# Nystromformer attention and a multiplicative feed-forward on one core: an earlier table load, constants split between two engines, later w_out loads on SyncE, and the first eighth of w3 x w_out in two kinds of products

## The chip, the core and the metric

The kernel runs on one core of a Trainium2 chip. The core has five engines with instruction streams of their own, which wait for each other through semaphores: TensorE (PE, matrix products), VectorE (DVE), ScalarE (ACT), GpSimd (POOL) and SyncE (SP, which issues loads and stores). The metric is the device time of one execution in microseconds; shorter is better.

## What is computed

Eight batches of eight heads with 576 rows of 64 go through a Nystrom attention with 32 landmarks; the result, as 4608 rows of 512, goes through a feed-forward in which two projections are multiplied.

```python
q_lm = q.reshape(B, H, m, S // m, D).mean(axis=3)      # m = 32 landmarks, S // m = 18 rows each
k_lm = k.reshape(B, H, m, S // m, D).mean(axis=3)
A, Bm, C = sm(q, k_lm), sm(q_lm, k_lm), sm(q_lm, k)    # softmax of scaled scores
Z = Bm.transpose(0, 1, 3, 2) / (norm1(Bm) * norm_inf(Bm) + 1e-06)
for _ in range(6):
    Z = 2 * Z - Z @ Bm @ Z
x = (A @ Z @ C @ v), heads side by side: 4608 x 512
a, b = x @ w1, x @ w2                                  # 512 -> 1024 each
out = ((a * b) @ w3) @ w_out                           # 1024 -> 1024 -> 512
```

The kernel forms w3 @ w_out (1024 x 512) once, so that each row then needs one product less.

## The kernel before, in words

**Tasks and an order written out.** The program is a list of some 1330 small tasks. Each has a name, an engine, a function that issues its instructions, and rings of buffers or banks that it takes and gives back. ORDER (L39 to L116) names every task once, with the buffer that it takes behind a colon; `run` (L149) issues the tasks in just that order. So ORDER fixes, for each engine, the sequence of its instructions: an engine that waits for one instruction does nothing that stands behind it. The costs and due times given with the tasks play no part any more once ORDER is written.

**The names.** The 64 heads are 16 quads n of four heads. Of a quad, `lq` n t (L599, GpSimd's queue) loads K (t = 0) and Q (t = 1); `T` (L429) transposes them on VectorE; the landmark means come from TensorE for quads 0 and 1 (`mp`, L450, with the identity `ident16`) and from GpSimd for the others (`ma`, `mb`); `mk` (L458) scales them on ScalarE, `lt` (L471) transposes them; `S` and `A` (L478, L527) are the scores, `sm`, `sw`, `sb`, `se`, `ct` and `ar`, `am`, `as`, `ae`, `au`, `an`, `aT` their softmax on VectorE, GpSimd and ScalarE. `sw` (L500) is a small matmul with the constant `swapneg`. Batches b of two quads then have `C`, `W`, `U`; groups i of batches have the iteration for Z (`N`, `x`, `y`, `Z`). `d`, `e`, `f` are the dense products of the feed-forward, `g`, `h`, `st` its end and the stores.

**w3 x w_out.** Both weights are split into a half-precision copy and a half-precision remainder, so that the product of the copies and two products of a copy with a remainder give the wanted exactness. w_out is loaded in four quarters `wf0` to `wf3` of four pieces each: the pieces marked s are issued by SyncE, those marked a by ScalarE (L380). Of each eighth c, `woh` (L312, ScalarE) is the copy and `wol` (L317, VectorE) the remainder. w3 comes in eight slabs `w3n` j of 512 KB; `tr` (L323) transposes half a slab into a PSUM bank, `wh` (L330, ScalarE) and `wl` (L337, VectorE) make copy and remainder. `mm` j c (L347) does the three products of slab j with eighth c, 192 matmuls of 512 columns in all, and `wo` j (L357) takes the sum out. The gates `gw` 0 to 3 (L363, GpSimd) copy one element of each w_out quarter; the loads of Q and K from quad 2 on and of w1 and w2 (`lw`) stand behind gw3, so that they start only when w_out is there.

**The start.** `zz` (L260) clears a tile, on which 30 warm-up matmuls (`wu0` to `wu4`, L263, six each) run. `ca`, `cb` and `cc` make the constants: `cb` on GpSimd the identity, `cc` (L272) on VectorE everything else in 24 instructions. On ScalarE the order is: the loads of w3n0a, wf0a, wf1a and the first piece of wf2a, then wh00, wh01, woh1, woh0, the second piece of wf2a, mk0, wf3a, woh2, woh3 and so on. ScalarE's table load stands ahead of its first activation, wh00. On VectorE: cc, tr00, T00, tr01, wl01, wl00, T01, wol0, wol1, lt0, T10, sm0, wol2, ar0. On TensorE: wu4, mp0, mm00, mm01, S0, A0, sw0, mm02, mp1, mm03.

The functions that the change touches, and what calls them, with the line numbers that the profile uses:

Of the kernel before, what the change touches and what calls it, by code (L numbers as in the profile page):

```python
# [39 lines left out]
w3n0a.0 w3n0.0:0 zz w3n0a w3n0 lq00:0 ca wu0:0 wf0a.0 wf0s.0 lq01 wf0a wf0s lq10:1 wf1a.0 wf1s.0 wf1a wf1s lq11  # L40
wf2a.0 wf2s.0 cb wf2s wu1:1 cc wf3s.0 wu2:2 wf3s tr00:3.0 wu3:4 T00:0 wh00 tr01:5 w3n1.0:1 wu4:6 wh01 wl01 woh1
gw0 w3n1.1 wl00 mp0:7 woh0 T01 wf2a wol0 mk0:0 w3n1.2 wol1 mm00:0 wf3a.0 mm01 lt0 wf3a T10:1 S0:1.2 woh2 gw1
w3n1 A0:4.6 sm0:0 woh3 wol2 sw0 ar0:0 mm02 w3n2.0:2 sb0 wol3 mp1:5 am0:1 woh4 gw2 w3n2.1 mm03 woh5 wol4 w3n2.2
mk1:1 T11 mm04 gw3 w3n2 wol5 as0 woh7 w3n3.0:0 lt1 woh6 mm05 wol7 w3n3.1 lq20:2 se00:0 A1:3.7 w3n3.2 wol6 ae0
lq21 w3n3 tr10:4.1 mm06 lq30:3 au0 wh10 lq31 S1:6.5 se01 mm07 lq40:0 wl10 lw10 tr11:1 mm10:2 lq41 ar1:1 wh11
w3n4.0:1 mm11 an0:0 w3n4.1 tr20:4.0 mm12 w3n4.2 am1:2 lw11 mm13 wh20 w3n4 bo0:0 wl11 lw00 T20:0 mm14 as1 wl20
mm15 sm1:3 mm20:3 ae1 ma2:0 tr21:7 mm16 ct0:0 sw1 w3n5.0:2 mm21 w3n5.1 sb1 T21 se10:1 mm17 w3n5.2 lq50:1 aT0:0
se11 mm22 w3n5 mb2 tr30:1.1 wh21 mm23 au1 wh30 wl21 bo1 N0:4.4 tr31:6 mm24 wl30 w3n6.0:0 lq51 mk2:0 mm25 w3n6.1
bt0 T30:1 lq60:2 mm26 w3n6.2 an1:1 no0:0 wh31 mm27 mm30:5 ct1:1 ma3:0 mm31 lt2 w3n6 wl31 A2:7.1 tr40:4.0 mm32
# [10 lines left out]
ct3:0 lv4 mb7 mm76 wq0 lv5.0:1 sb6 au5 se60:1 U000:3.7.0.1 lv5.1 U010:1.4 se61 lv5.2 am6:0 U011:2.5 uo0001 lv5  # L60
mm77 bo5 T71 uo0100 N1:6.3 uo0110 ct5:1 lq100:2 mk7:1 C1:7.1 bt1 an5:1 T80:0 no1:0 uo0111 ma8:0 uo0000 wo7 aT5:5
U001:2.5 lv6.0:2 lt7 co1:1.5 lv6.1 uo0011 S7:3.6 lv6.2 uo0101 sm7:1 as6 A7:0.5 lv6 uo0010 d010:1.7 lv7.0:3 T81
lv7.1 mb8 d000:4.2 ar7:1 e010:0 lv7.2 sw7 lv7 e000:1 T90:1 C2:1.0 ae6 am7:2 sb7 au6 lq101 mk8:0 f000:0 as7
x1_0:5 lv8.0:0 co2:0.3 d020:4.2 lv8.1 se70:0 lv8.2 lt8 lq110:3 d002:0.1 se71 y1_0:1 lv8 T91 ma9:0 e020:2
d030:3.5 lv9.0:1 e002:1 f010 lv9.1 x1_1:6 f002:1 e030:0 lv9.2 d011:4.0 f020 ae7 ct6:0 d012:7.1 bo6:0 an6:0
e011:1 y1_1:2 A8:3.2 e012:2 f030 d022:4.6 mb9 ar8:0 d032:7.5 f012 d001:2.3 e032:0 am8:6 e022:2 x1_2:1 f011
S8:7.4 y1_2:0 g00:0 f032 lq111 mk9:1 f022 lq120:0 x1_3:1 T100:0 lq121 d021:5.6 e001:1 sm8:8 ma10:0 g01 e021:0
f001 lt9 sw8 y1_3:1 d031:2.5 sb8 f021 se80:1 x1_4:3 T101 e031:2 S9:1.6 lq130:1 h0:0 au7 g30:7 mb10 st0.0 g31
y1_4:2 lv9 bo7 ct7:2 A9:2.0 h3:1 f031 Z1:3 se81 sm9:5 st3.0 g10:7 T110:1 an7:1 mk10:0 sw9 zo1:1 g11 as8 sb9
aT7:0 se90:0 lt10 W1:5 ar9:1 h1:2 W2:4 ma11:0 g20:3 wp1:1 ae8 wq1 T111 se91 U100:1.7.2.3 am9:4 wp2:0 g21 uo1000  # L70
aT6:1 uo1001 as9 wq2 U101:0.2 h2:3 ct9:1 U200:5.6.0.1 uo1010 au8 U210:1.7 mb11 uo2000 S10:4.3 uo2101 C3:0.5
sm10:9 ae9 bo8 ct8:3 uo2100 au9 uo2001 uo1011 an8:1 sw10 lv10.0:2 A10:7.1 mk11:1 co3:1.3 lv10.1 U211:6.2 lv10.2
sb10 an9:0 ar10:0 U111:0.5 uo2111 lv10 se100:0 lv11.0:3 am10:0 d200:2.1 ma12:0 bo9 lv11.1 uo1110 T120:0 d211:7.4
lv11.2 e200:1 lv11 se101 lt11 N2:0.2 T121 st1.0 uo2110 C4:2.3 bt2 uo1111 f200:2 as10 e211:0 no2:0 lq131 ae10
f211 mb12 U201:6.5 lv12.0:0 co4:0.1 U110:1.7 lv12.1 uo2010 A11:0.4 au10 lv12.2 uo2011 d201:2.3 lv12 uo1101
lv13.0:1 ar11:1 uo1100 d202:6.5 st2.0 d120:7.1 lq140:2 am11:7 e202:2 lv13.1 e201:1 lq141 st2 S11:0.4 f202:3
# [86 lines left out]
def kernel(  # L163
# [860 lines left out]
```

## Time and profile before

| | us |
|---|---|
| median of 3 runs | 271.43 (270.89 to 271.73) |
| profiled execution | 273.18 |
| its span, first to last instruction | 271.1 |
| TensorE busy | 256.1 |
| VectorE busy | 193.8 |
| ScalarE busy | 162.0 |
| GpSimd busy | 131.8 |

The loads move 37.33 MB in all; the mean granted TensorE clock is 0.986. In the rows of the profile PE is TensorE, PEld its weight loads, DVE VectorE, ACT ScalarE, POOL GpSimd, SP SyncE; a q behind a name is the engine's sequencer, which issues loads. Nearly all matmuls have line L243, that of a helper, so they are told apart by their tiles. The w_out quarters are loaded into tiles that later hold other things, and so are called u (wf0, wf1) and ab (wf2, wf3).

### The profile page before, as it was taken

What the parts mean: (1) busy time and instruction counts of PE and PEld (TensorE: products, weight loads), DVE (VectorE), ACT (ScalarE), POOL (GpSimd) and SP (SyncE); (2) the same over time, 40 slices, a digit from 0 to 9 for tenths busy, and PEclk for the clock granted to TensorE, in tenths of its full rate; (3) what the DMA queues carried; (4) which work ended last, traced back from release to release, by engine and by line L of the source; (5) the groups of instructions that cost most, each with busy time, mean ns of one, the idle gap of its engine ahead of it and who ended that gap; (6) DMA issues with size and microseconds to landing.
All of it is one profiled execution on the core that took longest, in us unless ns stands there. A gap on an engine that the chain in (4) does not pass through costs nothing.

```text
span 271.1 us, 9581 instructions
## 1 busy us (share of the span) xinstructions
PE 256.1 (94%) x3954; PEld 168.5 (62%) x3954; DVE 193.8 (71%) x470; ACT 162.0 (60%) x414; POOL 131.8 (49%) x147
## 2 busy tenths in 40 slices
PE   8569989999999999999999999999999999999992
PEld 3325434454558875679867556976857597666752
DVE  4659999999999999999899868744664076313330
ACT  0546364565576757989864898735024984593542
POOL 4007899999999999999788431000020000000000
PEclk9986999999999999999999999999999999999999
DMA  7998999999988967099643133023624050142455
GB/s 155 282 211 187 194 234 236 235 245 232 222 217 202 203 136 166 10 203 203 154 77 89 41 80 85 19 62 97 170 77 95 4 119 0 41 101 47 109 136 138
DMA packets 22668, 37.33 MB, mean 138 GB/s; under 512 B 3552, under 2 KB 7904, under 8 KB 22624
## 3 DMA queue, kind: packets, MB, share of 16 engines
q1 hardware_dynamic: 15920, 23.80, 34.9%
q0 software_dynamic: 5696, 11.54, 24.4%
q10 hardware_dynamic: 1008, 1.38, 1.8%
q8 instruction: 31, 0.51, 0.8%
q14 instruction: 13, 0.11, 0.1%
HBM read 38.80 MB, written 9.44 MB: 178 GB/s over the span
## 4 chain that ended last, share of the span: by engine, by line
PE 57%; DMA 15%; DVE 10%; POOL 10%; ACT 2%; issue 2%; SPq 1%; ACTq 0%; DVEq 0%; POOLq 0%
PE bank L243 57%; DMA w3n<-in_moe_w_dram 8%; POOL ls L439 3%; POOL ls L446 3%; DMA ab<-in_moe_w_out_dram 3%; DMA u<-in_moe_w_out_dram 2%; POOL ea L552 2%; DMA vb<-in_v_dram 2%; DVE bank L325 2%; DVE T L431 2%; DVE w3t L340 1%; DVE ea L540 1%; ACT lm L467 1%; SPq L306 1%; POOL nat L406 1%
## 5 line engine op out<-in xcount | busy, mean ns | idle before, releaser
L871 DVE TENSOR_TENSOR ab<-asb,bank 128x384 f16<-128x384 f16 x96 | 49.4, 544 | 33.0 <-ACT asb L865 32.3
L243 PE MATMUL bank<-aT,u 128*128 128x192 f16 x768 | 70.2, 246 | 1.0 <-issue 0.4
L243 PE MATMUL bank<-w,ab 128*128 128x512 f16 (+1 forms) x296 | 69.4, 374 | 0.0
L243 PEld LDWEIGHTS <-u 128*128 128x128 f16 x768 | 63.8, 98 | 8.4 <-issue 1.9
L865 ACT CAST asb<-bank 128x384 f16<-128x384 f32 x96 | 43.5, 486 | 27.7 <-PE bank L243 25.0
L243 PE MATMUL bank<-wo,w3t 128*128 128x512 f16 x192 | 47.7, 390 | 2.5 <-ACT wo L314 1.4
L243 PEld LDWEIGHTS <-ab 128*128 128x128 f16 x296 | 27.5, 99 | 25.6 <-issue 1.6
L446 POOL TENSOR_TENSOR ls<-ls 128x128 f32<-128x128 f32 (+2 forms) x56 | 40.9, 730 | 3.5
L790 ACT CAST u<-bank 128x512 f16<-128x512 f32 x64 | 33.4, 611 | 3.9 <-PE bank L243 3.9
L439 POOL TENSOR_TENSOR ls<-nat 128x1152 f32<-128x1152 f16 x14 | 33.3, 2378 | 2.8 <-ACT lm L467 1.9
L580 POOL TENSOR_TENSOR ah<-ea,tiny 128x576 f16<-128x576 f32 x16 | 18.6, 1166 | 32.5 <-DVE aT L589 28.4
L885 ACT ACTIVATE osb<-bank 128x512 f32<-128x512 f32 x35 | 21.2, 606 | 20.2 <-PE bank L243 20.1
L243 PEld LDWEIGHTS <-w3t 128*128 128x128 f16 x192 | 18.2, 102 | 23.6 <-issue 6.1
L431 DVE STREAM_TRANSPOSE T<-nat 128x576 f32<-128x576 f32 x32 | 24.0, 755 | 1.6 <-DMA nat<-in_k_dram 1.6
L552 POOL TENSOR_TENSOR ea<-ea,tiny 128x608 f32<-128x608 f32 x16 | 19.4, 1214 | 9.9 <-ACT ec L516 6.5
L516 ACT ACTIVATE ec<-bank,tiny 128x288 f32<-128x288 f32 x32 | 16.0, 501 | 8.0 <-DVE tiny L508 8.0
L243 PE MATMUL bank<-T 32*32 32x288 f16 (+1 forms) x320 | 18.6, 291 | 1.4 <-DVE T L473 1.0
L243 PE MATMUL bank<-vb,ecT 64*64 64x128 f32 x576 | 18.4, 272 | 0.0
L243 PEld LDWEIGHTS bank<-vb,ecT 64*64 64x64 f32 x576 | 16.6, 133 | 1.0 <-DVE tiny L566 0.4
L243 PE MATMUL bank<-xz 32*32 32x64 f32 (+1 forms) x768 | 16.4, 214 | 0.2 <-DVE xz L725 0.2
L243 PEld LDWEIGHTS bank<-xz 32*32 32x32 f32 x768 | 12.7, 104 | 6.2 <-issue 1.9
L243 PE MATMUL bank<-w,wT 64*32 64x512 f16 x512 | 16.1, 378 | 0.0
(77 smaller groups left out, 296.6 us busy)
## 6 DMA issues: line engine op xcount, KB each, us to landing
vb<-in_v_dram SPq DMA_DIRECT2D x64, 144.0 KB, 4.5
out_dram<-osb SPq DMA_DIRECT2D x70, 128.0 KB, 2.4
nat<-in_k_dram POOLq DMA_DIRECT2D x16, 288.0 KB, 7.3
nat<-in_q_dram POOLq DMA_DIRECT2D x16, 288.0 KB, 8.2
w3n<-in_moe_w_dram SPq DMA_DIRECT2D x30, 128.0 KB, 7.3
w<-in_moe_w_dram POOLq DMA_DIRECT2D x4, 512.0 KB, 13.9
u<-in_moe_w_out_dram SPq DMA_DIRECT2D x4, 128.0 KB, 7.2
u<-in_moe_w_out_dram ACTq DMA_DIRECT2D x4, 128.0 KB, 8.4
```

Of the source, the lines that this page charges most:

```text
L243: nc.tensor.matmul(out_, lhsT, rhs, start=start, stop=stop, **({} if pos is None else {"tile_position": pos}))
L325: nc.vector.transpose(out=bank(at(f"w3f{j}{h}")).rearrange("p (e g i) -> p g e i", e=4, g=4), in_=w3n[at(f"w3n{j}")].rearrange("p g (e x) ...
L431: nc.vector.transpose(out=Ts[at(f"T{n}")][:, GRP * t:GRP * t + GRP] .rearrange("p r l e -> p (r l e)").bitcast(FP32), in_=nats[at(f"nat{n} ...
L439: nc.gpsimd.tensor_tensor(out=l, in0=nat[:, :, 0:9, :], in1=nat[:, :, 9:18, :], op=ALU.add)
L446: nc.gpsimd.tensor_tensor(out=l[:, :, x:x + m, :], in0=l[:, :, x:x + m, :], in1=l[:, :, y:y + m, :], op=ALU.add)
L516: nc.scalar.activation(out=ecs[at(f"ec{n}")][:, hp, :], in_=two(f"pS{n}")[hp][:, 0:288], func=AXF.Exp, scale=SCALE, bias=t[:, 2 + hp:3 + h ...
L552: nc.gpsimd.tensor_tensor(out=ea, in0=ea, in1=tinies[at(f"ta{n}")][:, 0:19].unsqueeze(2).to_broadcast([128, 19, M]), op=ALU.subtract)
L580: nc.gpsimd.tensor_tensor(out=ahs[at(f"ah{n}")].rearrange("p g m r -> p g r m"), in0=eas[at(f"ea{n}")][:, 0:GRP, :].rearrange("p (g r) m - ...
L790: nc.scalar.copy(out=uu[at(f"u{b}{qd}")][:, wi, 512 * half:512 * half + 512], in_=bank(at(f"pU{b}{wi}{half}{qd}")))
L865: nc.scalar.copy(out=asb[at(f"as{b}{j}{ch}")], in_=d1_ps(b, j, ch)[0])
L871: nc.vector.tensor_mul(abts[at(f"ab{i // 2}")][:, 2 * j:2 * j + 2, CH * (i % 2):CH * (i % 2) + CH], asb[at(f"as{b}{j}{ch}")], d1_ps(b, j, ...
L885: nc.scalar.activation(out=osb[at(f"os{i}")], in_=bank(at(f"pE{i}")), func=AXF.Copy, scale=2.0 ** -12)
```

## The change

- A new task `tab` on ScalarE copies one column of the cleared tile, right after the third load issue, so that the table load comes there.
- `cc` keeps only the memsets (11 instructions); `cd` (VectorE) makes ident16; `ce` (GpSimd) makes `swapneg`, `unit64` and `minus2I` with 12 instructions. The users of these wait for the part that they need.
- wf2a and wf3a are issued by SyncE behind wf2s and wf3s; the second w3 slab and the V loads stand behind wf3a there.
- The first slab's products come apart: `mh` c is the product of the copies, `mm0` c the two others; both add into the same bank.
- One block of six warm-up matmuls goes (four blocks, 24 matmuls).
- ORDER is written anew from end to end. VectorE now begins zz, ca, cc, T00, cd, tr00, wl00, tr01, wol0, wol1, T01, wl01, lt0, T10, sm0, ar0, wol2; ScalarE w3n0a, wf0a.0, tab, wf0a, wf1a, wh00, woh0, woh1, wh01, mk0, woh2; TensorE mp0, mh0, mm00, mm01, S0, A0, mh1, mh2, mh3, sw0, mp1; GpSimd has ce between gw0 and gw1.

```diff
-    for x in range(5):
+    for x in range(4):
...
+    def table():
+        nc.scalar.activation(out=tabo, in_=aTs[0][:, 0:1], func=AXF.Copy, scale=1.0)
...
     def const_c():
-        nc.vector.tensor_copy(out=ident16, in_=ident)
         nc.vector.memset(blockneg, 0.0)
         nc.vector.memset(ones, 1.0)
         nc.vector.memset(kmask, 0.0)
...
+    def const_d():
+        nc.vector.tensor_copy(out=ident16, in_=ident)
+
+    def const_e():
+        for j in range(4):
+            o = 32 * (j ^ 1)
+            nc.gpsimd.tensor_scalar(out=swapneg[:, 32 * j:32 * j + 32], in0=ident[:, o:o + 32],
+                                    scalar1=-SCALE, scalar2=None, op0=ALU.mult)
+        for j in range(4):
+            r = slice(32 * j, 32 * j + 32)
+            nc.gpsimd.tensor_scalar(out=unit64[r, :].rearrange("p (a m) -> p a m", a=2),
...
+            nc.gpsimd.tensor_scalar(out=minus2I[r, :], in0=ident[r, r], scalar1=-2.0, scalar2=None,
                                     op0=ALU.mult)
...
+    def w34_first(c):
+        def fn():
+            mm(bank(at("pw0")), w3t[at("w3t0")][:, 0, c].rearrange("p g i -> p (g i)"), wo[:, 0, c, :],
+               start=(c == 0), stop=False)
+        return fn
+
+    def w34_rest(c):
+        def fn():
+            ps = bank(at("pw0"))
+            hi, lo = (w3t[at("w3t0")][:, i, c, :, :].rearrange("p g i -> p (g i)") for i in range(2))
+            mm(ps, hi, wo[:, 1, c, :], start=False, stop=False)
+            mm(ps, lo, wo[:, 0, c, :], start=False, stop=(c == 7))
+        return fn
...
-            load(f"w3n{j}", "SP", 4 if j else 2, 0.47, load_w3(j, nc.sync, 0), [f"~w3n{j - 1}", "~wf3s"] if j else [],
+            load(f"w3n{j}", "SP", 4 if j else 2, 0.47, load_w3(j, nc.sync, 0), [f"~w3n{j - 1}", "~wf3a"] if j else [],
...
+                            if x == "a" and c >= 4:
+                                e, eng, before = "SP", nc.sync, f"wf{c // 2}s"
+                            elif x == "s" and c == 6:
+                                before = "wf2a"
...
+                if j == 0:
+                    add(f"mh{c}", "PE", 0.215, w34_first(c),
+                        deps=[f"woh{c}", f"wh0{c // 4}", f"mh{c - 1}" if c else "wu3"],
...
+                    add(f"mm0{c}", "PE", 0.43, w34_rest(c),
+                        deps=[f"woh{c}", f"wol{c}", f"wh0{c // 4}", f"wl0{c // 4}", f"mm0{c - 1}" if c else "mh0"]
+                        + (["mh7"] if c == 7 else []),
...
```

More of the change, by code (lines that the diff above doesn't have):

```diff
@@ L39 @@
 ORDER = """
[L40 to L49, printed above, removed]
@@ L60 @@
[L60 to L64, printed above, removed]
@@ L115 @@
-st33.0 g350:1 st33 h34:2 st34.0 g351:6 h350:0 st34 h351 st3501 st3511 st3510 st3500
+w3n0a.0 w3n0.0:0 zz w3n0a w3n0 lq00:0 ca wu0:0 cc wf0a.0 wf0s.0 lq01 tab wf0s cb wf1s.0 lq10:1 wf1s lq11 wf2s.0
+wf0a wf2s wf1a.0 wu1:1 wf1a wf2a.0 wu2:2 wf2a wu3:3 T00:0 cd tr00:4.0 wf3s.0 wh00 wl00 tr01:5 woh0 gw0 wf3s ce
+mp0:6 woh1 wol0 wh01 mh0:7 wol1 mm00 mk0:0 wf3a.0 T01 mm01 wl01 lt0 T10:1 woh2 gw1 wf3a S0:0.1 A0:2.3 woh3 sm0:0
+mh1 mh2 ar0:0 w3n1.0:1 mh3 sw0 mp1:4 wol2 w3n1.1 am0:1 w3n1.2 woh4 gw2 w3n1 wol3 w3n2.0:2 woh5 mh4 wol4 mm02
@@ new lines @@
+w3n2.1 mm03 wol5 w3n2.2 mh5 woh7 gw3 w3n2 mm04 T11 as0 mm05 w3n3.0:0 woh6 wol7 w3n3.1 mk1:1 mh6 lq20:2 wol6
+w3n3.2 lq21 sb0 mm06 tr10:6.1 w3n3 se00:0 lq30:3 mh7 lt1 mm07 wh10 tr11:5 lq31 S1:2.3 ae0 wl10 lw00 w3n4.0:1
+A1:4.0 wo0 w3n4.1 au0 lq40:0 mm10:6 wh11 w3n4.2 lq41 mm11 w3n4 ar1:1 bo0:0 an0:0 mm12 tr20:7.0 mm13 lq50:1 am1:2
+wh20 se01 wl11 as1 tr21:0 mm14 wl20 lw10 wh21 w3n5.0:2 mm15 w3n5.1 aT0:0 ae1 ma2:0 mm20:4 wl21 w3n5.2 mm16 w3n5
+sm1:3 mm17 au1 mm21 mb2 ct0:0 mm22 bo1 mm23 T20:0 mm24 tr30:1.1 sw1 T21 wh30 N0:5.4 mm25 tr31:7 an1:1 mk2:0 mm26
@@ L600, in quad_tasks @@
                  [] if t else [("nat", f"nat{n}", 3)], [], (f"q{n}", 0.1 * t), "lq", (1.55, 0.23))
[L601 removed]
+        load(f"lv{n}", "SP", 4, 0.47, load_v(n), [f"~lv{n - 1}"] if n else ["~wf3a"], [("vb", f"vb{n}", 1)], [], (f"v{n}", 0.0), "lv", (0.48, 0.12))
         loads = [f"lq{n}0", f"lq{n}1"]
```

164 lines of the change are left out of this document (87 added, 77 removed).

## The prediction, made before the changed kernel ran

> **What bounds the kernel now.** I read the page first, for who is busy and who is on the chain.
>
> ```profile
> span 271.1 us, 9581 instructions
> PE 256.1 (94%) x3954; PEld 168.5 (62%) x3954; DVE 193.8 (71%) x470; ACT 162.0 (60%) x414; POOL 131.8 (49%) x147
> PE 57%; DMA 15%; DVE 10%; POOL 10%; ACT 2%; issue 2%; SPq 1%; ACTq 0%; DVEq 0%; POOLq 0%
> ```
>
> TensorE (PE) is busy for 94% and holds 57% of the chain. That is a mean over unlike stages, so I cut the span into stretches (busy time and count per engine, then the granted clock, the DMA share and GB/s).
>
> ```profile
> 9.00:12.00 3.00, 0.66 (x10) 0.44 (x9) 2.34 (x4) 2.88 (x5) 0.18 (x1) 1.00 1.11 286
> 14.00:20.00 6.00, 3.54 (x29) 1.25 (x28) 3.26 (x10) 2.45 (x8) 0.28 (x2) 0.81 1.08 197
> 20.00:25.35 5.35, 5.35 (x30) 3.21 (x29) 5.35 (x10) 3.91 (x12) 3.25 (x6) 0.58 0.88 202
> 25.35:116.00 90.65, 87.85 (x1426) 51.26 (x1425) 88.21 (x210) 57.81 (x165) 86.98 (x93) 1.00 0.90 193
> 116.00:266.30 150.30, 149.44 (x2422) 108.22 (x2422) 88.96 (x212) 93.81 (x226) 37.96 (x38) 1.00 0.40 92
> ```
>
> From 116 us on TensorE is the bound: 149.44 of 150.30 us, while VectorE (DVE) has time to spare. From 25 to 116 us three engines are full at once: VectorE 88.21, TensorE 87.85 and GpSimd (POOL) 86.98 of 90.65 us. Only before 20 us does everybody wait: TensorE works 3.54 of 6.00 us there, VectorE 3.26, GpSimd 0.28. The chain of waits, in order of time, says which of the three leads in the middle:
>
> ```profile
> 8.02 6.89 DMA ab<-in_moe_w_out_dram
> 14.93 5.87 DMA w3n<-in_moe_w_dram
> 25.35 0.71 DVE bank L325
> 30.36 1.21 POOL ea L552
> 116.26 21.47 PE bank L243 x400
> ```
>
> It runs through loads until 25 us, then through VectorE and GpSimd, then through TensorE. So a gain at the start reaches the end if VectorE's and GpSimd's full stretches begin earlier. I therefore price the change by when VectorE reaches its first transpose of the second w3 slab (tr10, L325, at 25.35), and when GpSimd begins its work.
>
> **The change part by part.** The start, in the timeline (start, duration, what; in brackets the idle time before and what ended it):
>
> ```profile
> 1.23 8.02 PE L243 MATMUL bank<-aT 128*128 128x512 f16 x30 [1.23 <-DVE aT L261]
> 6.56 0.72 DVE L325 STREAM_TRANSPOSE bank<-w3n 128x512 f32<-128x512 f32 x1
> 8.37 1.28 ACT L332 ACT_TABLE_LOAD   x1 [8.37 <-DMA u<-in_moe_w_out_dram]
> 8.86 0.78 DVE L431 STREAM_TRANSPOSE T<-nat 128x576 f32<-128x576 f32 x1 [1.57 <-DMA nat<-in_k_dram]
> 9.66 1.21 ACT L332 ACTIVATE w3t<-bank 128x512 f16<-128x512 f32 x2
> 10.90 1.29 DVE L340 SCALAR_TENSOR_TENSOR w3t<-bank,w3t 128x512 f16<-128x512 f32 x2 [0.66 <-ACT w3t L332]
> 10.80 0.18 POOL L365 COPY gates<-u 128x1 f32<-128x1 f32 x1 [6.87 <-DMA u<-in_moe_w_out_dram]
> 11.59 1.17 PE L243 MATMUL bank<-nat,ident 128*128 128x128 f16 x18 [2.34 <-DVE w3t L340]
> 13.89 0.22 ACT L465 ACTIVATE lm<-bank 128x64 f16<-128x64 f32 x1 [1.98 <-DMA u<-in_moe_w_out_dram]
> 14.97 0.35 DVE L473 STREAM_TRANSPOSE T<-lm 128x160 f32<-128x160 f32 x1 [0.92 <-ACT lm L467]
> 15.90 0.80 DVE L497 TENSOR_REDUCE tiny<-bank 128x1 f32<-128x288 f32 x2
> 17.42 0.32 ACTq L298 DMA_DIRECT2D ab<-in_moe_w_out_dram  x1
> 17.86 1.15 ACT L314 ACTIVATE wo<-u 128x512 f16<-128x512 f32 x2 [2.92 <-DMA w3n<-in_moe_w_dram]
> 18.52 0.69 DVE L319 SCALAR_TENSOR_TENSOR wo<-u,wo 128x512 f16<-128x512 f32 x1 [1.83 <-ACT wo L314]
> 22.10 0.18 POOL L365 COPY gates<-ab 128x1 f32<-128x1 f32 x1 [2.25 <-DMA ab<-in_moe_w_out_dram]
> 22.24 1.21 POOL L552 TENSOR_TENSOR ea<-ea,tiny 128x608 f32<-128x608 f32 x1
> 22.55 1.45 DVE L319 SCALAR_TENSOR_TENSOR wo<-ab,wo 128x512 f16<-128x512 f32 x1
> 23.40 0.58 POOL L406 DMA_DIRECT2D nat<-in_k_dram  x1
> ```
>
> *ScalarE's loads of w_out to SyncE, and the early table load.* ScalarE (ACT) starts late not for its own work: it issues loads, and a load issue waits for an earlier landing. The chain shows this (landing at 8.02 + 6.89 = 14.91, next issue at 14.93); in ORDER the thirteenth load of SyncE and ScalarE waits for the fifth, so eight are in flight. The issue at 17.42 (wf3a) holds woh2 until 17.86, 2.92 us, and through it VectorE, 1.83 us; the one before mk0 costs 1.98 and 0.92 us. After the change ScalarE issues six loads, the last two (13th and 14th in the new ORDER) behind the 5th's and 6th's landing near 8.0, so it is free near 8.7. The table load, 1.28 us, then lies at about 2 to 3 us beside the warm-up; delaying wf0a's issue costs nothing, since that one waits for an eighth-earlier landing anyway. Both are hidden until wh00, whose input comes later.
>
> *T00 and cd ahead of tr00.* Before, tr00 ran at 6.56, in time in which VectorE otherwise idled. Now it stands behind T00, which waits for the first K load (8.86). T00, cd and tr00 thus end near 10.5; wh00 takes 0.60 (half of 1.21), and wl00, now ahead of tr01, waits for it. This is the change's cost: 0.70 + 0.23 us of work and about 0.75 of idle time on VectorE, where 0.66 was.
>
> *The sum on VectorE.* From T00 to tr10 are now 25.35 - 8.86 = 16.49 us. Away go the three waits, 0.66 + 0.92 + 1.83 = 3.41. In come tr00 0.70, cd 0.23, the wait for wh00 0.75, and one for the scores behind lt0 that I take as 0.25 (sm0, at 15.90, began 0.93 us after lt0; T10 fills 0.7 of it). lt1 (0.27 us by starts) moves behind tr10: no gain. 16.49 - 3.41 + 1.93 = 15.01, so VectorE does the same work **1.5 us** sooner.
>
> *Loads.* Nothing is added to what is loaded; the order changes. By the last landing of w_out (gate at 22.10) the same 24 pieces of 128 KB have come: four of w3's first slab, sixteen of w_out, four of its second slab. Now w_out's are first, so its last piece lands four pieces sooner. A piece takes 128 KB / 231 GB/s = 0.57 us (17-18 us below), so 2.3 us: gw3 near 19.8. Queued behind wf3a on SyncE stand the second slab's loads: all landed near 22, while VectorE wants them at 23.6. Then as0 begins near 20 instead of 22.24 and lq20's issue near 21.1 instead of 23.40. GpSimd gains 2.3 us; VectorE, with 1.5, decides.
>
> *Constants split.* Twelve small operations go from VectorE to GpSimd (ce), between gw0 and gw1:
>
> ```profile
> L281 DVE TENSOR_SCALAR unit<-ident 32x64 f32<-32x64 f32 x4 | 0.7, 184 | 0.0
> L287 DVE TENSOR_SCALAR swapneg<-ident 128x32 f32<-128x32 f32 x4 | 0.7, 177 | 0.0
> L284 DVE TENSOR_SCALAR minus2I<-ident 32x32 f32<-32x32 f32 x4 | 0.7, 165 | 0.0
> L446 POOL TENSOR_TENSOR ls<-ls 128x128 f32<-128x128 f32 x28 | 12.7, 455 | 2.2
> ```
>
> VectorE loses 2.1 us, but from 4 to 6.5 us, where it would idle: worth 0. GpSimd has no such row. Bounds: 12 x 0.17 = 2.0 us and 12 x 0.455 = 5.5 us; I take 3, nearer to the small VectorE rows. Behind it wait gw1 to gw3, as0 and lq20; from gw0 near 10.8 it ends by 16.3 at the longest, ahead of 19.8: hidden either way.
>
> One L319 above lasts 1.45 us instead of its median 0.68, exactly beside GpSimd's L552. I leave that in the sum once, as now. [...]
>
> *The first eighth as mh and mm0.* The same 24 matmuls; the eight copy products no longer wait for the remainders. TensorE idles there, so this only fills gaps: 0.
>
> *One warm-up block less.* Six matmuls go, 6 x 8.02 / 30 = 1.6 us at most, that compute nothing. The price is in the third rival.
>
> *The rewritten order.* I cannot price each swap. From 25.35 to 116 VectorE idles 90.65 - 88.21 = 2.4 us: no order takes more than that out of it. On the other side I allow as much. I take 0.
>
> The profiled execution took 273.18 us (span 271.1 and 2.1 around it), 0.6% above the median of 271.43. The sum, 273.18 - 1.5 = 271.7, is taken over as a difference: 271.43 - 1.5 = **269.9 us**.
>
> **The rivals.** *The loads take the gain.* From 25 us on the DMA engines are full:
>
> ```profile
> 25.35:60.00 34.65, 32.73 (x340) 15.36 (x339) 33.96 (x77) 18.19 (x52) 32.72 (x36) 1.00 1.10 225
> 14.00:17.00 3.00, 2.08 (x26) 0.83 (x25) 1.78 (x5) 0.94 (x5) 0.10 (x1) 1.00 1.10 184
> 17.00:18.00 1.00, 0.14 (x2) 0.07 (x2) 0.00 (x0) 0.14 (x1) 0.00 (x0) 0.85 1.09 231
> 18.00:24.00 6.00, 5.32 (x26) 3.01 (x26) 5.48 (x10) 3.93 (x11) 2.09 (x5) 0.50 0.92 198
> 24.00:25.00 1.00, 1.00 (x5) 0.37 (x4) 1.00 (x3) 1.00 (x4) 1.00 (x2) 0.74 1.00 249
> ```
>
> If w3's slabs and the Q and K loads decide, only the slack before can be won: (1.10 - 0.88) / 1.10 x 5.35 = 1.1 us at most, half of it likely, since lq20 now comes beside the third and fourth slab: 270.9 us. For it speaks the share of 1.10; against it, that VectorE waits for almost nothing in that stretch (33.96 of 34.65).
>
> *The new order packs better.* All 2.4 us of VectorE's later idle time come out too: 271.43 - 3.9 = 267.5 us. For it, in the new ORDER wq0 stands ahead of S6 and A6, which opens TensorE's long final stretch sooner. Against it, three full engines.
>
> *Slower: TensorE's clock falls in the gap after the shorter warm-up.* Place: 8 to 12 us. Now the warm-up ends at 1.23 + 8.02 = 9.25 and the gap is 2.34 us (row at 11.59), with the clock held. Six matmuls less end near 7.8, and mp0 still waits for the first Q load: a gap of 3.8 us. The clock fell to 0.50 at about 17.7, after 14 to 17.7 in which TensorE was busy for 2.2 us, and returned near 24.5, after some six busy us. If it falls at 11 and returns only there, the cold time grows from 0.3 + 6.0 + 0.5 = 6.8 to 13.6 us, at half rate 3.4 us of TensorE work. [...] It turns the result if TensorE, not VectorE, sets the pace until 116 us: 271.43 - 1.5 + 3.4 = 273.3 us. Against it, TensorE is cold in part of that time already, and idles 2.8 us from 25 to 116.
>
> **How the numbers follow.** What a measurement here can tell from no change is about 0.3%, 0.8 us. Chances: forecast (269.0 to 270.6) 0.42; better packing 0.13; loads take the gain 0.20; clock, or an order that waits more, 0.25. So faster 0.55, same 0.20, slower 0.25. The range goes from the packing rival's 267.5 to just under the clock rival's 273.3, 273.1; what lies beyond holds some 0.15 to 0.2.
>
> **What would show it.** Right: tr10's first transpose near 23.6 instead of 25.35; no wait of ScalarE for a load beyond 9 us; as0 near 20; VectorE without a wait of over 0.5 us from 13 us on. The cost of moving tr00 shows as the first L332 after 10.4. The load rival shows as VectorE waiting for w3n between 25 and 60; the clock rival as a clock of 0.50 before 17 us. Wrong would make me above all a first K load later than 8.8 us, on which all of VectorE's start now hangs, or a stall in the rewritten middle that this start cannot show.

## The result and the profile after

The changed kernel took 270.73 us (median of 20 executions, 268.68 to 272.63), beside 271.93 us for the kernel before (20 executions). The ratio is **0.9954 (95% interval 0.9935 to 0.9973)**: 1.2 us faster, between 0.7 and 1.8. A second measurement gave 0.9941 (0.9914 to 0.9969). The forecast was 269.9 us, a gain of 1.5 us out of 271.43.

The profiled execution took 268.93 us and is the second fastest of the 20, so its times flatter the change. The head of its page, and the chain's shares:

```profile
span 267.2 us, 9564 instructions
PE 254.8 (95%) x3948; PEld 167.4 (63%) x3948; DVE 191.2 (72%) x458; ACT 161.5 (60%) x415; POOL 136.9 (51%) x159
PE 67%; POOL 14%; DVE 7%; ACT 5%; issue 3%; DMA 2%; DVEq 0%; POOLq 0%; ACTq 0%
```

TensorE has hardly less to do, and DMA has left the chain: 2% where it held 15%. The stretches, cut as in the prediction (busy us and count of TensorE, its weight loads, VectorE, ScalarE, GpSimd; granted clock, DMA share, GB/s):

```profile
9.00:12.00 3.00, 1.63 (x21) 1.26 (x22) 2.34 (x5) 2.48 (x7) 2.38 (x8) 1.00 1.11 279
14.00:20.00 6.00, 5.42 (x54) 2.95 (x46) 6.00 (x12) 3.07 (x9) 2.65 (x6) 1.00 1.11 223
20.00:25.35 5.35, 3.98 (x34) 1.75 (x34) 5.22 (x12) 3.24 (x8) 4.64 (x9) 1.00 1.12 208
25.35:116.00 90.65, 88.99 (x1485) 52.54 (x1483) 87.86 (x208) 58.80 (x170) 87.26 (x90) 1.00 0.91 198
116.00:262.40 146.40, 146.21 (x2334) 105.81 (x2330) 85.34 (x206) 90.33 (x215) 35.45 (x37) 1.00 0.39 90
```

Only the rows of the start are new. From 14 to 20 us VectorE now works 6.00 of 6.00 us, where it worked 3.26, and TensorE 5.42 instead of 3.54. From 25.35 to 116 us VectorE is busy for 87.86 us where it was 88.21: the same stretch, entered earlier. The rows of the timeline that answer to those of the prediction:

```profile
1.21 7.44 PE L245 MATMUL bank<-aT 128*128 128x512 f16 x24 [1.21 <-DVE aT L266]
2.15 1.28 ACT L256 ACT_TABLE_LOAD   x1 [2.15 <-issue]
3.60 1.43 ACTq L313 DMA_DIRECT2D u<-in_moe_w_out_dram  x2
7.62 0.78 DVE L474 STREAM_TRANSPOSE T<-nat 128x576 f32<-128x576 f32 x1 [5.61 <-DMA nat<-in_k_dram]
8.32 0.18 DVE L287 CAST ident<-ident 128x128 f16<-128x128 f32 x1
8.42 0.72 DVE L340 STREAM_TRANSPOSE bank<-w3n 128x512 f32<-128x512 f32 x1
9.17 0.60 ACT L347 ACTIVATE w3t<-bank 128x512 f16<-128x512 f32 x1 [5.52 <-DVE bank L340]
9.80 0.69 DVE L355 SCALAR_TENSOR_TENSOR w3t<-bank,w3t 128x512 f16<-128x512 f32 x1 [0.66 <-ACT w3t L347]
10.21 1.17 PE L245 MATMUL bank<-nat,ident 128*128 128x128 f16 x18 [1.56 <-DMA nat<-in_q_dram]
11.03 1.28 DVE L334 SCALAR_TENSOR_TENSOR wo<-u,wo 128x512 f16<-128x512 f32 x2
11.10 0.74 POOL L299 TENSOR_SCALAR minus2I<-ident 32x32 f32<-32x32 f32 x1
13.51 0.32 DVE L516 STREAM_TRANSPOSE T<-lm 128x160 f32<-128x160 f32 x1
14.18 0.29 POOL L299 TENSOR_SCALAR minus2I<-ident 32x32 f32<-32x32 f32 x1
14.41 0.79 DVE L540 TENSOR_REDUCE tiny<-bank 128x1 f32<-128x288 f32 x2
18.12 0.41 POOL L394 COPY gates<-ab 128x1 f32<-128x1 f32 x1 [2.07 <-DMA ab<-in_moe_w_out_dram]
18.50 1.67 POOL L595 TENSOR_TENSOR ea<-ea,tiny 128x608 f32<-128x608 f32 x1
19.71 1.60 DVE L334 SCALAR_TENSOR_TENSOR wo<-ab,wo 128x512 f16<-128x512 f32 x2
20.11 0.63 POOL L449 DMA_DIRECT2D nat<-in_k_dram  x1
21.41 0.73 DVE L340 STREAM_TRANSPOSE bank<-w3n 128x512 f32<-128x512 f32 x1
```

VectorE's first transpose of the second slab (tr10) stands at 21.41 instead of 25.35. Between T00 and tr10 the VectorE rows show one wait, the 0.66 us for wh00. The two stretches from T00 to tr10, the first of the kernel before:

```profile
8.86:25.35 16.49, 11.15 (x80) 5.85 (x79) 13.09 (x23) 9.49 (x24) 4.01 (x9) 0.79 1.02 226
```

and of the kernel after:

```profile
7.62:21.41 13.79, 9.18 (x83) 4.83 (x82) 13.10 (x25) 7.42 (x20) 8.15 (x20) 1.00 1.10 249
```

VectorE is busy in it for as long as before, 13.09 and 13.10 us, although tr00 and cd have come in and lt1 has left; its idle time fell from 3.40 to 0.69 us. So of the 3.94 us by which tr10 is earlier, 2.70 come from waits that went, and 1.24 because T00 began at 7.62 instead of 8.86: the first K load landed earlier in this execution. TensorE ends here:

```profile
257.71 4.72 PE L245 MATMUL bank<-w,ab 128*128 128x512 f16 x29
```

That is 262.43, and 241.02 us behind tr10; before it was 266.30 - 25.35 = 240.95. The whole difference lies ahead of tr10.

### The profile page after: what moved, and what is told of

Its sections match the earlier page's. It is cut to its first block, busy times and chain, and to the rows that moved or that the text cites. A ratio compares the mean times of both kernels' runs of the same rounds, so it can differ in the third digit from the quotient of the medians.

```text
span 267.2 us, 9564 instructions
## 1 busy us (share of the span) xinstructions
PE 254.8 (95%) x3948; PEld 167.4 (63%) x3948; DVE 191.2 (72%) x458; ACT 161.5 (60%) x415; POOL 136.9 (51%) x159
## 4 chain that ended last, share of the span: by engine, by line
PE 67%; POOL 14%; DVE 7%; ACT 5%; issue 3%; DMA 2%; DVEq 0%; POOLq 0%; ACTq 0%
PE bank L245 67%; POOL ls L489 5%; POOL ls L482 4%; DMA nat<-in_k_dram 2%; ACT lm L510 2%; POOL ea L595 2%; DVE bank L340 1%; DVE wo L334 1%; POOL nat L449 1%; ACT u L833 1%; DVE tiny L609 1%; DVE T L474 1%; POOL w L467 1%; ACT ec L559 1%; DVE tiny L589 1%
## 5 line engine op out<-in xcount | busy, mean ns | idle before, releaser
L245 PE MATMUL bank<-aT,u 128*128 128x192 f16 x768 | 69.4, 246 | 0.0
L245 PE MATMUL bank<-wo,w3t 128*128 128x512 f16 x192 | 46.3, 380 | 2.7 <-DVE wo L334 2.1
L833 ACT CAST u<-bank 128x512 f16<-128x512 f32 x64 | 34.0, 616 | 3.0 <-PE bank L245 3.0
L245 PEld LDWEIGHTS <-w3t 128*128 128x128 f16 x192 | 17.3, 98 | 24.5 <-issue 5.1
L595 POOL TENSOR_TENSOR ea<-ea,tiny 128x608 f32<-128x608 f32 x16 | 19.8, 1241 | 9.6 <-DVE tiny L589 6.0
L347 ACT ACTIVATE w3t<-bank 128x512 f16<-128x512 f32 x16 | 9.5, 593 | 12.3 <-DVE bank L340 12.1
L245 PE MATMUL bank<-w,wT 64*32 64x512 f16 x512 | 16.8, 378 | 0.0
```

Of the source, the lines that this page charges most:

```text
L245: nc.tensor.matmul(out_, lhsT, rhs, start=start, stop=stop, **({} if pos is None else {"tile_position": pos}))
L347: nc.scalar.activation(out=w3t[at(f"w3t{j}")][:, 0, 4 * h:4 * h + 4].rearrange("p e g i -> p (e g i)"), in_=bank(at(f"w3f{j}{h}")), func=A ...
L595: nc.gpsimd.tensor_tensor(out=ea, in0=ea, in1=tinies[at(f"ta{n}")][:, 0:19].unsqueeze(2).to_broadcast([128, 19, M]), op=ALU.subtract)
L833: nc.scalar.copy(out=uu[at(f"u{b}{qd}")][:, wi, 512 * half:512 * half + 512], in_=bank(at(f"pU{b}{wi}{half}{qd}")))
```

## The experiments

The **theory**: the time is decided by when VectorE reaches tr10, because from there VectorE leads until 116 us; the gain comes from ScalarE's load issues that no longer hold VectorE's inputs back. **Rivals**: the rewritten order in the middle gains or loses something of its own; TensorE (by its clock) or GpSimd leads; the loads' place is beside the point and another part brings the gain. Each profile below is of one execution; each ratio is of medians, with the runs of the kernel before on the same chip.

| kernel | ratio (95% interval) | T00 | tr10 | TensorE's end | end - tr10 |
|---|---|---|---|---|---|
| before | 1 | 8.86 | 25.35 | 266.30 | 240.95 |
| after | 0.9954 (0.9935 to 0.9973) | 7.62 | 21.41 | 262.43 | 241.02 |
| after, again | 0.9941 (0.9914 to 0.9969) | 8.62 | 22.95 | 263.95 | 241.00 |
| after, five warm-up blocks | 0.9925 (0.9899 to 0.9952) | 8.01 | 21.81 | 262.86 | 241.05 |
| after, loads on ScalarE again | 0.9960 (0.9941 to 0.9979) | 7.92 | 22.63 | 263.62 | 240.99 |
| after, five blocks, tr00 first | 0.9957 (0.9933 to 0.9981) | 8.73 | 21.67 | 263.06 | 241.39 |
| before, loads on SyncE | 0.9889 (0.9860 to 0.9917) | 9.12 | 22.71 | 263.34 | 240.63 |
| the same again | 0.9915 (0.9887 to 0.9943) | 8.95 | 22.53 | 263.38 | 240.85 |
| before, early table load | 0.9949 (0.9926 to 0.9973) | 7.67 | 23.93 | 264.49 | 240.56 |
| before, both of these | 0.9905 (0.9873 to 0.9938) | 7.47 | 21.40 | 262.45 | 241.05 |
| before, loads on SyncE, four blocks | 0.9935 (0.9910 to 0.9961) | 8.54 | 22.90 | 263.09 | 240.19 |

The last column is the first finding: in eleven profiles, with the old order and the new one, TensorE ends 240.2 to 241.4 us behind tr10. Where the rewritten order is used it is 241.0 to 241.4, with the old one 240.2 to 241.05. For the change itself, with 241.02 and 241.00 against 240.95, the middle and the end were neither gained nor lost.

**The loads alone.** The kernel before, with wf2a and wf3a on SyncE right behind wf2s and wf3s.

```diff
+                            if x == "a" and c >= 4:
+                                e, eng = "SP", nc.sync
```

> The kernel before with one part of the change alone: wf2a and wf3a are issued by SyncE, right behind wf2s and wf3s, and ScalarE issues none of them; order, constants and warm-up as before. Theory (VectorE's and GpSimd's start): ScalarE is not held at mk0 and woh2, so VectorE's waits of 0.92 and 1.83 us go and the last w_out gate, 22.1 us, comes 2 us or more sooner; 1 to 2 us faster than before, as much as the whole change or more, because tr00 stays ahead of T00. Rival (the new order is what pays): the start moves but the old order behind it can't use it, within 0.5 us of before. Rival (clock): a gain only where the clock stays up in 16 to 25 us.

It took 269.35 us beside 272.33: 3.0 us less, more than the 1 to 2 expected and more than the whole change. The stretch from T00 to tr10 in its profile:

```profile
9.12:22.71 13.59, 9.76 (x86) 5.07 (x85) 12.72 (x24) 8.02 (x22) 4.09 (x9) 1.00 0.95 226
```

Idle are 13.59 - 12.72 = 0.87 us instead of 3.40. This one edit removes the waits; the table task, the split constants and the new order are not needed for it. But it moves the table load as well: with no load issue at 8.02 ahead of it, ScalarE's table load ran at 5.37 instead of 8.37, and wh00 at 7.31 instead of 9.66.

**The same again**, on another chip, with more executions.

> The kernel before with nothing but the last two loads of w_out that ScalarE issued put on SyncE: the first run of it gave 0.9889 (0.986 to 0.9917) from six executions, lower than the whole change with 0.9954 and 0.9941. If that holds, 0.987 to 0.991 here, and its interval ends below 0.9935. Rival, that the six executions were luck: 0.992 to 0.995, and nothing that the change adds costs anything.

The ratio is 0.9915 and the interval ends at 0.9943, not below 0.9935: the first expectation is missed by a little. The two medians, 269.45 and 269.35 us, agree; what differs is the kernel before beside them, 271.91 and 272.33. So the loads alone bring 2.5 to 3.0 us, against the change's 1.2 and 1.35. That the change is slower than its best part is likely, but the intervals touch.

**The loads back on ScalarE**, in the changed kernel.

```diff
-                            if x == "a" and c >= 4:
-                                e, eng, before = "SP", nc.sync, f"wf{c // 2}s"
-                            elif x == "s" and c == 6:
-                                before = "wf2a"
```

> The changed kernel with the a pieces of wf2 and wf3 on ScalarE again, at their places in its order; all else as changed. Theory: ScalarE is held again by load issues, the last w_out gate comes 2 us or more later, and the gain is lost: 1 to 3 us slower than the changed kernel, at or above the time of before. Rival (new order pays): less than 0.5 us slower.

It took 271.06 us, 0.996, nearly that of the change: the expected loss did not come. In the changed kernel the place of these loads is worth at most a few tenths of a per cent. The same edit is worth 2.5 to 3 us in the old order and next to nothing in the new one: the parts do not add up. The stretch from T00 to tr10 tells why:

```profile
7.92:22.63 14.71, 10.26 (x81) 4.80 (x80) 13.47 (x25) 7.54 (x20) 7.40 (x20) 0.88 1.06 245
```

VectorE idles for 14.71 - 13.47 = 1.24 us, not 3.40. In the new order woh2 stands between ScalarE's last two issues (13.78 and 15.65 in this profile) and no longer behind both, so it runs at 14.33 instead of 17.86, and VectorE's wol2 finds it done. So most of the waits ahead of tr10 can be taken out in two ways, by moving the loads or by the order, and the change does both. The order was not run by itself; the early table load alone leaves 2.95 us of idle time (16.26 less 13.31 in the next profile).

**The early table load alone**, in the kernel before.

```diff
+    def table():
+        nc.scalar.activation(out=tabo, in_=aTs[0][:, 0:1], func=AXF.Copy, scale=1.0)
+
+    add("tab", "ACT", 1.4, table)
```

> The kernel before with the early table load alone. Theory: the table load, 1.28 us, leaves the path to wh00, but wh00 then still stands behind the load issue of wf2a.0 near 8.0; wh00 near 8.4 instead of 9.66, yet mm00, mk0 and woh2 stay held by the later loads: 0 to 0.5 us faster. Rival: if the first activation sets the start, 1.3 us faster.

The ratio is 0.9949: 1.6 us less than the 272.33 beside it, where the theory gave at most 0.5. Its stretch from T00 to tr10 does not show why:

```profile
7.67:23.93 16.26, 11.43 (x93) 5.80 (x91) 13.31 (x23) 8.80 (x23) 4.03 (x9) 1.00 1.11 240
```

16.26 us are only 0.23 less than before, with the waits still in it; what moved is T00, at 7.67, by an earlier first K load. The first K load landed at 7.2 to 8.7 us in ten profiles with the early table load (mean 7.98), and at 8.5 to 9.1 in four without it (mean 8.85). The two groups overlap, and I have no mechanism for it: ScalarE's w_out issues behind the table load come at 3.67 and 4.61, no later than the 3.86 and 4.86 of before. The clock is another candidate: 3 of the 12 executions had a mean below 0.995, of the 23 of the kernel before beside them 19; but the three took 270.5 us on average, the other nine 271.0. What the table load's place does to the time is measured, why stays open.

**Both of these**, in the kernel before.

```diff
 # the two edits above together
```

> The kernel before with two parts of the change, loads on SyncE and the early table load; order behind them as before. Theory (both take ScalarE's waits out of VectorE's start, and they add up): alone they gave 3.0 and 1.4 us; together 3.5 to 4.5 us faster than before, 0.984 to 0.987. Rival (they take out the same wait): 3.0 us, 0.989.

0.9905, between the two runs of the loads alone (0.9889 and 0.9915); the 0.984 to 0.987 of the theory did not come. VectorE idles from T00 to tr10 for 0.87 us (13.93 less 13.06), as with the loads alone: both take out the same waits. The profile has the earliest T00 and tr10 of the old order (7.47 and 21.40), but the medians do not show a gain on top.

**Five warm-up blocks in the changed kernel.**

```diff
-    for x in range(4):
+    for x in range(5):
```

> The changed kernel with the fifth warm-up block again (30 matmuls). Theory: the gap before mp0 gets shorter and nothing else; within 0.4 us of the changed kernel. Rival (the clock decides): if the shorter warm-up lets the clock fall in most executions, this one keeps it and is about 1 us faster, with a higher mean granted clock (0.996 or more instead of 0.991).

The ratio is 0.9925, some 0.3% below that of the change; the intervals overlap. The mean granted clock tells it more plainly: 0.996 to 1.0 in all six executions, whereas 14 of the change's 20 had 0.990 to 0.994, and 7 of the 12 of its second measurement. I read a mean below 0.995 as a fall to half ahead of the last microseconds: the nine profiles without such a fall have means of 0.995 to 1.0, the five with one, of some 3.4 us in four of them and of 6.8 in that of before, 0.986 to 0.993.

**The change again, with its own profile.**

> The changed kernel itself, once more, beside the others. If its gain of 1.2 us holds, 0.993 to 0.998 of before again. Theory (clock): its profile shows the granted clock at 0.50 for one stretch of about 3.4 us between 10 and 18 us, as in most executions of it (mean clock 0.991), which its first profile did not have. Rival: the clock is up throughout and the time is near 270.7 us all the same.

0.9941, as expected. The fall of the clock that I expected of the profile is not in it: the granted clock is 1.00 in the stretch below and 0.995 on average, so no profile of the change itself shows the fall. This profile, at 270.46 us, is the typical one: the first K load landed a microsecond later, and tr10 stands at 22.95. The stretch:

```profile
8.62:22.95 14.33, 8.80 (x81) 4.60 (x79) 13.67 (x24) 7.42 (x20) 8.94 (x22) 1.00 1.07 243
```

Idle is again 0.66 us; VectorE's work is 0.57 us longer, mostly because GpSimd's first subtraction lay beside another pair of L334, which took 2.30 us (1.28 in the first profile; the later pair took 1.25 here and 1.60 there).

**Four warm-up blocks with the loads on SyncE**, in the kernel before.

```diff
-    for x in range(5):
+    for x in range(4):
```

> The kernel before with w_out's later pieces on SyncE (3.0 us faster than before by itself) and with four warm-up blocks instead of five. Theory (the shorter warm-up lets the clock fall): 0.5 to 1.2 us slower than with five blocks, about 0.992 to 0.993 of before. Rival (the warm-up does not matter): 0.989 as with five.

0.9935 instead of 0.9889 and 0.9915 with five blocks, and a mean clock below 0.995 in 11 of 12 executions, where none of the 18 with five blocks was below 0.995. It took 270.05 us, 0.6 to 0.7 more than with five (269.45 and 269.35); the intervals overlap. Here the profile caught the fall. TensorE's rows:

```profile
1.23 7.13 PE L243 MATMUL bank<-aT 128*128 128x512 f16 x24 [1.23 <-DVE aT L261]
11.22 1.68 PE L243 MATMUL bank<-nat,ident 128*128 128x128 f16 x18 [2.86 <-DMA nat<-in_q_dram]
```

and the stretches, whose third number from the right is the granted clock:

```profile
10.00:12.00 2.00, 0.78 (x12) 0.81 (x13) 1.41 (x3) 1.59 (x3) 0.00 (x0) 0.92 1.10 274
12.00:14.00 2.00, 2.00 (x13) 1.10 (x11) 1.74 (x3) 1.06 (x6) 0.61 (x1) 0.50 1.08 270
14.00:16.00 2.00, 2.00 (x23) 0.69 (x22) 1.22 (x3) 1.01 (x2) 0.00 (x0) 0.73 1.10 264
```

From 0.92 in 10 to 12 us the fall lies near 11.7, 3.3 us behind the end of the warm-up at 8.36, with TensorE at work again for the last 0.5 us of that. In the kernel with the loads back on ScalarE the clock fell too; its TensorE rows:

```profile
1.21 7.43 PE L245 MATMUL bank<-aT 128*128 128x512 f16 x24 [1.21 <-DVE aT L266]
10.69 1.17 PE L245 MATMUL bank<-nat,ident 128*128 128x128 f16 x18 [2.05 <-DMA nat<-in_q_dram]
11.70 0.38 PE L245 MATMUL bank<-wo,w3t 128*128 128x512 f16 x1
```

and its stretches:

```profile
12.00:14.00 2.00, 1.63 (x5) 0.40 (x3) 2.00 (x4) 1.38 (x6) 1.76 (x4) 0.57 1.07 296
14.00:16.00 2.00, 1.71 (x22) 0.65 (x22) 1.87 (x5) 0.63 (x1) 0.83 (x3) 0.58 1.11 257
```

The fall lies near 12.3, 3.6 us behind the warm-up's end at 8.64, with 1.4 us of matmuls in that time and a gap of only 2.05 us. What sets the fall off these runs do not show: in neither profile was TensorE idle for the whole of that time.

**Five blocks and tr00 ahead of T00**, in the changed kernel.

```diff
-... wu3:3 T00:0 cd tr00:4.0 wf3s.0 ...
+... wu3:3 wu4:2 cd tr00:4.0 T00:0 wf3s.0 ...
```

> The changed kernel with the fifth warm-up block again and with cd and tr00 ahead of T00, as in the order before. Theory (tr00 behind T00 costs 0.7 to 1.5 us of VectorE's start, the warm-up 0.8): 1.5 to 2 us faster than the changed kernel, about 0.988 to 0.990, level with the kernel before plus loads on SyncE. Rival (the rewritten order further on costs what is missing): 0.992 as with the fifth block alone.

0.9957: a miss of both expectations, although the clock held in all twelve executions (0.995 to 1.0). In the profile the transpose does go into idle time, as it did before the change:

```profile
5.19 0.73 DVE L340 STREAM_TRANSPOSE bank<-w3n 128x512 f32<-128x512 f32 x1 [2.04 <-DMA w3n<-in_moe_w_dram]
8.73 0.78 DVE L474 STREAM_TRANSPOSE T<-nat 128x576 f32<-128x576 f32 x1 [2.81 <-DMA nat<-in_k_dram]
```

The stretch from T00 to tr10 shrinks to 12.94 us, from 13.80 with five blocks alone. But T00 came at 8.73 instead of 8.01, and the median is not lower. Why 0.9 us saved behind T00 do not show in twelve executions is not settled.

**A delay on VectorE** right behind tr11, in the changed kernel: five memsets whose output nothing uses.

```diff
+        for _ in range(5):
+            nc.vector.memset(pad, 0.0)
```

> The changed kernel with five memsets of 128x288 more on VectorE right behind the second transpose of the second w3 slab (some 1.4 us; nothing uses their output). In the changed kernel TensorE's end lies 241.02, 241.00 and 241.05 us behind VectorE's first transpose of that slab (three profiles). My theory, that VectorE sets the pace from there to 116 us: the distance grows by most of what the memsets last, 1.1 to 1.5 us, to 242.1 to 242.5. Rival, that GpSimd or TensorE sets it and VectorE has slack: it stays within 241.0 to 241.4.

```profile
21.63 0.73 DVE L346 STREAM_TRANSPOSE bank<-w3n 128x512 f32<-128x512 f32 x1 [0.52 <-DMA w3n<-in_moe_w_dram]
23.22 2.00 DVE L305 MEMSET pad<- 128x288 f32 x5
258.92 6.23 PE L246 MATMUL bank<-w,ab 128*128 128x512 f16 x36
```

The memsets took 2.00 us, more than the 1.4 that they were sized for. TensorE ends at 265.14, 243.51 us behind tr10 instead of 241.0: 2.5 us for 2.0. But the clock fell too in this execution, at 26.4 us, where it did not in the profiles of the change:

```profile
25.00:60.00 35.00, 34.01 (x290) 15.53 (x290) 33.95 (x76) 16.79 (x48) 31.46 (x33) 0.95 1.12 233
```

A clock of 0.95 over 35 us is one of 0.50 for 3.5 us, in which TensorE, busy throughout, loses some 1.7 us of work. The next run adds just that much to TensorE, and 0.6 us of it reach the end. Even with that taken off, 1.9 of the 2.0 us of VectorE's delay reach the end.

**A delay on TensorE**, seven matmuls more ahead of mm10, whose result the next product overwrites.

```diff
+            for _ in range(7 if (j, c) == (1, 0) else 0):
+                mm(ps, wo[:, 0, 0, 0:128], wo[:, 0, 0, :])
```

> The changed kernel with seven matmuls of 512 columns more on TensorE ahead of the first product of the second w3 slab (some 1.5 us; the product that follows starts its bank anew). Theory that VectorE sets the pace: the distance from VectorE's first transpose of that slab to TensorE's end stays within 0.5 us of 241.0. Rival, that TensorE sets it from there on, as its share of 94 to 95% and the clock rival of the prediction suppose: it grows by 1.3 us or more, to 242.3.

```profile
24.20 1.67 PE L245 MATMUL bank<-wo 128*128 128x512 f16 x7
```

TensorE ends at 263.65, 241.61 us behind tr10 (22.04): 0.6 us for 1.67, a tenth above my bound. Some 1.1 us of slack is there. The clock held (1.00 from 8 to 116 us).

**A delay on GpSimd** behind its first subtraction (as0), one addition.

```diff
+        nc.gpsimd.tensor_tensor(out=pad, in0=pad, in1=pad, op=ALU.add)
```

> The changed kernel with one addition of 128x704 more on GpSimd behind its first subtraction (some 1.4 us; nothing uses its output, and one memset of that tile stands on VectorE ahead of the first K transpose, in time in which it waits). Theory that VectorE alone sets the pace: the distance from VectorE's first transpose of the second w3 slab to TensorE's end stays within 0.5 us of 241.0. Rival, that GpSimd sets it together with VectorE (87.3 and 87.9 of 90.65 us busy): it grows by 1 us or more.

```profile
20.54 2.77 DVE L340 SCALAR_TENSOR_TENSOR wo<-ab,wo 128x512 f16<-128x512 f32 x2
20.96 1.80 POOL L304 TENSOR_TENSOR pad<-pad 128x704 f32<-128x704 f32 x1
```

The clock fell here as well, at 23.1 us, for about 3.4 us:

```profile
21.00:25.00 4.00, 1.64 (x4) 0.55 (x4) 4.00 (x7) 1.55 (x4) 4.00 (x6) 0.77 1.03 186
25.00:60.00 35.00, 34.43 (x314) 15.80 (x312) 33.80 (x76) 18.03 (x52) 33.12 (x36) 0.98 1.10 229
```

The end is at 265.33, 242.03 us behind tr10 (23.30): 1.0 us for 1.80, between the two expectations, and up to 0.6 of it can be the clock's. So it does not decide whether GpSimd leads in part. Beside the addition, the two w_out remainders (L340 in this kernel, L334 in the changed one) took 2.77 us (1.60 in the profile of after); that, and a first K load that landed 0.86 us later, is why tr10 itself is late here.

Of the three engines that are full from 25 to 116 us, then, VectorE's delay reaches the end whole or nearly (1.9 to 2.5 of 2.0 us), GpSimd's with a quarter to a half (0.4 to 1.0 of 1.8), TensorE's with a third (0.6 of 1.67), each in one execution. GpSimd's own instructions show it too. Its second subtraction stands 5.26 us behind tr10 in the profile of after, 7.60 with VectorE's delay, 5.89 with GpSimd's own and 5.25 with TensorE's; its eleventh, near 115 us, 93.44, 95.78, 94.04 and 93.66. So VectorE's delay moves GpSimd at once and for the whole stretch. The theory stands: VectorE leads there, and the others follow with about a microsecond of slack.

## Why the prediction was right, point by point

- **What decides the time: right.** The prediction priced everything by tr10. The last column of the table and the delay on VectorE show that this was the right place.
- **ScalarE's waits: right, but not only by the loads.** The idle time of 3.40 us fell to 0.69, by the loads' move alone to 0.87, and with the loads back on ScalarE it is still only 1.24: the rest of the change, by its rows the order, takes most of the waits out too, which the prediction did not see. ScalarE was done with its last issue at 5.03 (3.60 + 1.43), not 8.7: its last two issues, at 3.60 and 4.71, followed the landings of SyncE's two pieces of the first slab (3.58 and 4.69) and not landings near 8.0. That changes nothing, since wh00 waits for tr00.
- **T00 and cd ahead of tr00: right in kind.** The wait for wh00 was 0.66 us (forecast 0.75), cd took 0.10 of VectorE's time by starts (8.32 to 8.42; forecast 0.23).
- **The sum from T00 to tr10: 15.01 forecast, 13.79 and 14.33 measured.** In the first, the wait of 0.25 behind lt0 did not come (the rows at 13.51 and 14.41 have no idle time); lt1, 0.27 us, which I counted as no gain, left the stretch, while the distance from tr10 to the end stayed at 241.0; the L334 beside GpSimd cost 0.45 us less; cd and wh00 0.13 and 0.09 less. Together 1.19 of the 1.22 us.
- **T00 at 8.86: wrong.** I took the first K load as given, and all of VectorE's start hangs on it, as I had named among what could go wrong. It landed at 7.59 and 8.59 in the change's profiles: it went the other way.
- **The table load's delay of wf0a and wf1a: right.** ScalarE's last two issues come at 3.60 and 4.71, before at 3.86 and 4.86. But the place of the table load is not worth nothing, as forecast: alone it brought 0.5%.
- **Why the gain is still no larger than forecast: in part luck.** The stretch from T00 to tr10 shrank by 2.2 to 2.7 us, not 1.5, and tr10 came 2.4 to 3.9 us sooner, yet the medians are 1.2 and 1.35 us apart. The profiled execution of before, from which the prediction took all its rows, lies 1.25 us above the median of its 20 (273.18 to 271.93), the change's first one 1.8 below its own. The change's second profile lies at its median, and its 2.40 us less those 1.25 are 1.15, what the medians show. What made the profiled execution of before so long is open, since it is the only one; its clock was at 0.50 from 17.7 to 24.5 us. So the prediction priced too small a gain and took it off a median that the profile did not stand for, and the two nearly cancel.
- **The clock rival: in part.** I gave it 3.4 us, for a fall at 11 us that lasts until 24.5; both times were estimates, and no run shows a fall that long there. Of the falls profiled with four warm-up blocks, the two right behind the warm-up came near 11.7 and 12.3 and were over some 3.4 us later (1.00 from 16 us on in both), at half rate 1.7 us of TensorE work each. By their means the clock fell in 21 of the change's 32 executions. Those took 270.8 us on average, the 11 others 270.1, with wide scatter; with five blocks the median is 0.3% lower. Both put its price at about 0.8 us, but five blocks with tr00 first kept the clock and gained nothing (0.9957), so the price is likely and not shown. The seven matmuls tell why it is less than 3.4: of TensorE's delay only a third reaches the end. Some 0.5 to 1 us of the distance to the loads alone stay unexplained.
- **The gap after the warm-up: wrong in size.** I put the end of the warm-up at 7.8 and mp0 at 11.59, a gap of 3.8 us. It ended at 8.65 (1.21 + 7.44), and mp0 came at 10.21, since the first Q load landed earlier too: 1.56 us in this profile, 2.01 in the second.
- **Loads and GpSimd: right in direction.** gw3 came at 18.12 and 18.72 (forecast 19.8), as0 at 18.50 and 18.89 (20), the first K load of quad 2 was issued at 20.11 and 20.51 (21.1). The rival that the loads take the gain did not hold in these profiles, but it is close: with tr10 due before 21.63, the VectorE-delay kernel waited 0.52 us for w3n.
- **ce: hidden, but longer.** From 9.55 to 14.47 it lasted 4.9 us, not 3, within the bounds of 2.0 and 5.5. gw1 waited for it until 14.53, gw2 and gw3 did not.
- **Better packing: no.** VectorE's idle time from 25.35 to 116 us is 2.8 us, not less than 2.4.

## What to carry to other kernels

Look for load issues that wait on a compute engine's queue. In the kernel before, wf3a's, which went out only at 17.42, kept ScalarE from woh2 for 2.92 us and through it VectorE from wol2 for 1.83; moving ScalarE's last four issues to SyncE brought 2.5 to 3.0 us, as much as anything tried here. In the new order the same move is worth next to nothing, where woh2 no longer stands behind both of the last issues. A change of many parts should be run part by part; here one part alone was at least as good as the whole, and a part that looked harmless, one warm-up block less, went with a mean clock below 0.995 in 21 of the change's 32 executions (none of 6 with five blocks). One profile need not stand for the median: compare the two before a gain is read off it. And to know which of several full engines leads, delay each by a known time and see how much of it reaches the end, with an eye on the clock of that run.

## What the runs showed of the hardware that was not expected

- **Side by side with VectorE, GpSimd's operations took longer too.** Beside wol0 and wol1 (11.03, 1.28 us for two, 1.25 before) GpSimd's operations of ce got longer: 0.74 us for the 32x32 one at 11.10, 0.29 at 14.18, where no such instruction of VectorE runs. wol0 had begun first, at 11.03. With as0 both took longer: as0 1.67 us (1.21 before), and the L334 beside it 1.00 of the 1.60 us, where the median of the eight is 0.68. Why the one or the other gets longer, these runs do not show.
- **The first K load varies.** It landed anywhere from 7.2 to 9.1 us in fourteen profiles; for a kernel whose first real work waits for it that is as much as the whole effect of the change.
- **The clock fell where TensorE was not wholly idle**: in the two profiles above, 3.3 and some 3.6 us behind the end of the warm-up, with 0.5 and 1.4 us of matmuls in that time; a gap of 2.01 us held it in one profile of the change, one of 2.05 did not in the kernel with the loads back on ScalarE.
